# Loading the second chunk of gate's weights one job earlier, in a retention and SwiGLU kernel on one core

## The chip, the cores and the metric

The kernel runs on one core of one Trainium2 chip. The time is device microseconds of one execution; the figure for a kernel is the median of several executions. TensorE is called PE in the profile, its weight loads PEld, VectorE DVE, ScalarE ACT, GpSimd POOL, and the engine that issues most DMAs SP.

## What is computed

The reference is a retention block (8 batches, 8 heads, 576 positions, 64 per head) whose output, laid out as 4608 tokens by 512, goes through an RMS norm and a SwiGLU feed-forward of width 1536.

```python
scores = scale * np.matmul(q, k.transpose(0, 1, 3, 2))
Dmat = np.where(rel >= 0, gamma[:, None, None] ** rel[None, :, :], 0.0)
attn_out = np.matmul(scores * Dmat[None], v)
x = attn_out.transpose(0, 2, 1, 3).reshape(B * S, H * D)
rms = np.sqrt(np.mean(x * x, axis=-1, keepdims=True) + 1e-06)
xn = x / rms * rms_g
g = xn @ w_gate
out = (g * (1 / (1 + np.exp(-g))) * (xn @ w_val)) @ w_out
```

All arithmetic is float32, but the three weight matrices arrive as 64-bit floats. The kernel rounds them to float32 itself.

## The kernel before

**Stages.** The attention is cut into jobs: one pair of heads of one batch, or of a part of one batch. Jobs 0 to 3 cover batch 0, jobs 4 to 7 the first 192 positions of batch 1. `start()` (L977) does these eight jobs, and then the feed-forward of the first two blocks of 384 tokens with plain matmuls (`up_plain`, L640; then `across`). After that, ten further blocks are computed with a seven-product scheme, among which the remaining attention jobs are slipped in. All of the change is in `start()`.

**One job.** In the loop over `j` in `start()`, `slot(j)` issues, in this order: PE's values of job `j-1` (L390), scores and states of job `j` (L307, L329), VectorE's weighting `ret` (L342) and running sums (L364, L366), and then the carried part of job `j-1` on PE (L412) with its result into `x` on VectorE (L435). Then `turn(j+1)` transposes the next job's q and k on PE (L247, L241) and copies them out on ACT (L252); `scale_v` scales v on ACT (L285); `square` (ACT L477) and `gather` (DVE L487) collect the sum of squares of the tokens. Job 5 ends with `norm_1(0)`: matmuls `ms` (PE L499), `r` (DVE L504) and a power on POOL (L505); then `diagonals` (DVE L547). Job 6 ends with `norm_2(0)`: `rb` (PE L562) and four L564 on VectorE, which give block 0's normalised `x`. The order written in the source is the order on every engine. A small memset `tick` on POOL (L401) stands between PE's values and carried parts of each job.

**Loads.** SP issues all loads of jobs 0 to 7 ahead of the job loop, job by job: q (L169), k and v (L177, two DMAs each), and for the first jobs the tails (L210). Eight semaphores are used in turn by SP's DMAs, so each of them is issued only once the eighth before it has landed. `load_chunks(n)` (L857 issues) loads weight chunks up to number `n`, in between.

**Weights.** A chunk is 512 rows by 256 columns of gate's or val's weights, 1 MB of 64-bit words. Chunks 0 and 1 are the two halves of the first third of gate, 2 and 3 those of val, and so on; after twelve of these come six of `w_out`. A chunk is first put in a spare place (in `w_out`, which is not yet in use, or in `w_gate`), and is then rounded on VectorE and ACT: `exponent` (DVE L874), then three passes on ACT (L890), which `act()` issues one at a time; the mantissa in three operations (DVE L901, L906, and L911, which needs the last ACT pass and ends the use of the spare place); and `join` (DVE L919), after which the chunk can be used. `rounding()` is a generator that goes through these operations chunk by chunk, one to a step. `weights(n)` takes `n` steps of it. Its step after L911 of chunk `i` also calls `load_chunks(i + 5)`, for chunk 1 that is chunks 4 and 5. For chunks from the second on, the exponent of the following chunk is taken ahead, before the join or before the mantissa, if its load has been issued.

Before the job loop three steps are taken, for chunk 0. In the loop, the numbers of steps by job are written by hand. Steps 4 and 5 end chunk 0; 6 to 9 are L874, L901, L906 and L911 of chunk 1; 10 is L874 of chunk 2; 11 is L919 of chunk 1.

**First matmuls of the feed-forward.** `up_plain(0, 0, 0)` has four groups of matmuls (L652, 128x384, four matmuls or eight records each). The first two read chunk 0, the last two chunk 1. Behind the first group stand values and carried part of job 7, its square and `gather`, and `weights(2)`; behind the second `norm_1(1)`, behind the third and fourth the rest of block 1's norm.

Of the kernel before, what the change touches and what calls it, by code (L numbers as in the profile page):

```python
# [41 lines left out]
def kernel(  # L42
# [11 lines left out]
    nc = tc.nc  # L54
# [104 lines left out]
    def load_first(j, tails):  # L159

        b, hp, *_ = jobs[j]
        d = st[j]
        tiles = tiles_of(j)[1]
        room = h_of[0].rearrange("p f t -> p (f t)")
        part = room[:, j * 4 * P : j * 4 * P + tiles * P]
        d["q"] = part.rearrange("p (e t d) -> p e t d", e=2, d=D)
        nc.sync.dma_start(  # L169
            out=part.rearrange("p (e t) -> p e t", e=2),  # L170
            in_=q[b, 2 * hp : 2 * hp + 2, : tiles * P].rearrange("e (p t) d -> p e (t d)", p=P),
        )
        for nm, src in (("k", k), ("v", v)):
            t = first_places[nm][j][:, : tiles * P].rearrange("p (c e d) -> p c e d", e=2, d=D)
            d[nm] = t
            for e in range(2):
                nc.sync.dma_start(  # L177
                    out=t[:, :, e],
                    in_=src[b, 2 * hp + e, : tiles * P].rearrange("(c p) d -> p c d", p=P),
                )  # L180
            for n in (0, 1) if nm == "k" else (2,):
                load_tails(b, n, tails)
# [50 lines left out]
    def turn(j):  # L233

        d = st[j]
        n = tiles_of(j)[1]
        for nm in "qk":
            ps = bank(f"turn_{j}_{nm}")
            for c in range(n):
                if nm == "k":  # L240
                    nc.tensor.transpose(  # L241
                        out=ps[:, c * P : c * P + P],
                        in_=d["k"][:, c].rearrange("p e d -> p (e d)"), identity=ident,
                    )
                    continue
                for e in range(2):
                    nc.tensor.matmul(  # L247
                        ps[side(e), c : n * P : n], lhsT=d["q"][:, e, c], rhs=ident,
                        start=True, stop=True,
                    )  # L250
            t = d[nm + "T"] = att.tile([P, S], F32, tag=nm + "T", name=f"{nm}T_{j}")
            nc.scalar.copy(out=t[:, : n * P], in_=ps[:, : n * P])  # L252
        if jobs[j][3] < NC:
            return
        last = bank(f"turn_{j}_t")
        for i, nm in enumerate("qk"):
            o = slice(i * TAIL, i * TAIL + TAIL)
            nc.tensor.transpose(
                out=last[:, o], in_=d[nm + "t"].rearrange("p e d -> p (e d)"),
                identity=ident[:TAIL, :TAIL],  # L260
            )
        for i, nm in enumerate("qk"):
            o = slice(i * TAIL, i * TAIL + TAIL)
            nc.scalar.copy(out=d[nm + "T"][:, NFULL * P :], in_=last[:, o])
# [13 lines left out]
    def scale_v(j):  # L278
        d = st[j]
        hp = jobs[j][1]  # L280
        i0, i1 = tiles_of(j)
        for e in range(2):
            tails = [d["vt"][:, e]] if "vt" in d else []
            for t in [d["v"][:, i0:i1, e]] + tails:
                nc.scalar.activation(  # L285
                    out=t, in_=t, func=AF.Copy, scale=gv[: t.shape[0], hp, e : e + 1]
                )
# [154 lines left out]
    def slot(j, rest=True):  # L442

        if j > len(jobs):
            return
        if rest and j > 0:
            values(j - 1)
        if j < len(jobs):
            scores(j)
            states(j)  # L450
        if j < len(jobs):
            weigh(j)
        if j < 2 * NHP:
            sums(j)
        if rest and j > 0:
            carried(j - 1)
        if 2 * NHP <= j < len(jobs):
            sums(j)
# [16 lines left out]
    def square(u, c):  # L475
        t = temp(f"sq_{u}_{c}")
        nc.scalar.activation(out=t, in_=x_of[u][:, c], func=AF.Square)  # L477
        return t

    def gather(u, c, sq):  # L480

        if c == NHP - 1 and u > 2:
            nc.vector.scalar_tensor_tensor(
                out=t_of[u], in0=t_of[u], scalar=EPS * DM / P, in1=sq, op0=ALU.add, op1=ALU.add
            )
        elif c:
            nc.vector.tensor_tensor(out=t_of[u], in0=t_of[u], in1=sq, op=ALU.add)  # L487
        else:
            t_of[u] = sq
# [5 lines left out]
    def norm_1(u):  # L495

        ms = bank(f"ms_{u}")
        for s in range(NS):
            nc.tensor.matmul(  # L499
                ms[:, s : s + 1], lhsT=t_of[u][:, s * P : s * P + P], rhs=mean_w,  # L500
                start=True, stop=True,
            )
        r = tmp.tile([P, NS], F32, tag="r", name=f"r_{u}", bufs=1)
        nc.vector.tensor_scalar(out=r, in0=ms[:, :NS], scalar1=EPS, scalar2=None, op0=ALU.add)  # L504
        nc.gpsimd.tensor_tensor(out=r, in0=r, in1=mhalf.to_broadcast([P, NS]), op=ALU.pow)  # L505
        t_of[u] = r
# [36 lines left out]
    def diagonals(u):  # L543
        r = t_of[u]
        t_of[u] = temp(f"diag_{u}")
        for s in range(NS):
            nc.vector.tensor_scalar(  # L547
                out=t_of[u][:, s * P : s * P + P], in0=ident, scalar1=r[:, s : s + 1],
                scalar2=None, op0=ALU.mult,
            )  # L550
# [290 lines left out]
    def spare(i):  # L841

        return i % 4 if i < n_up else LATER[i - n_up]

    def load_chunk(i, queue):
        dst, src, rws, cols = chunks[i]
        if src.dtype != F32:
            n = dst.shape[1]
            cols = slice(2 * (cols.start or 0), 2 * cols.stop if cols.stop else None)
            src = src.bitcast(U32)  # L850
            at = spare(i)
            dst = free[:, : 4 * DM] if at == 3 else (
                w_out[:, 4 * at : 4 * at + 4].rearrange("p c f -> p (c f)")
            )
            dst = words_of[i] = dst.bitcast(U32).rearrange("p (c f) -> p c f", c=n)
            waits_at[at] = i
        queue.dma_start(out=dst, in_=src[rws, cols].rearrange("(c p) f -> p c f", p=P))  # L857
        there_at[i] = now + 3 if now else 0

    def load_chunks(n, queue=nc.scalar):  # L860

        nonlocal n_loads
        while n_loads < min(n, len(chunks)) and waits_at.get(spare(n_loads)) is None:
            load_chunk(n_loads, queue)
            n_loads += 1
# [21 lines left out]
    def act(n=0, chunk=-1):  # L887

        while acts and (n > 0 or acts[0][0] <= chunk):
            nc.scalar.activation(func=AF.Relu, **acts.pop(0)[1])  # L890
            n -= 1
# [70 lines left out]
    def weights(n):  # L962

        for _ in range(n):
            next(steps, None)
# [11 lines left out]
    def start():  # L977
# [5 lines left out]
        def table(i, queue):  # L983
            t, values_ = tables[i]
            src = nc.inline_tensor(values_, name=t.tensor.name + "_table")
            queue.dma_start(out=t, in_=src.ap())
# [12 lines left out]
        for j in range(2 * NHP):  # L999
            load_first(j, {0: range(2), 1: range(2, H)}.get(j))  # L1000
            if j == 1:
                table(3, nc.sync)
            load_chunks((1, 1, 1, 1, 2, 2, 2, 3)[j], nc.sync)
        table(4, nc.sync)
        nc.sync.dma_start(out=rms_g, in_=moe_rms_g.rearrange("(c p) -> p c", p=P))
        load_chunks(4, nc.sync)
# [20 lines left out]
        for j in range(2 * NHP):  # L1027
            slot(j)
            if j + 1 < 2 * NHP:
                turn(j + 1)  # L1030
            if squares:
                gather(*squares.pop())
            for i in ((1,), (2,), (3,), (4, 5), (6,), (7,), (), ())[j]:
                scale_v(i)
            if j:
                u, c = divmod(j - 1, NHP)
                squares.append((u, c, square(u, c)))
            act(1)
            if j == 5:
                norm_1(0)  # L1040
            elif j == 6:
                norm_2(0)
            weights((2, 0, 0, 1, 1, 1, 1, 0)[j])
            if j == 4:
                gather(*squares.pop())
            elif j == 5:
                diagonals(0)
            act(1)
# [130 lines left out]
```

## Time and profile before

| | |
|---|---|
| median of 9 executions | 1136.57 us |
| lowest and highest | 1135.36 and 1137.64 us |
| the profiled execution | 1136.57 us, span 1134.8 us |
| granted PE clock, mean over the span | 0.994 |
| PE busy | 1116.2 us, 98% |
| VectorE busy | 732.8 us, 65% |
| ACT busy | 258.7 us, 23% |
| DMA | 126.73 MB, mean 112 GB/s |

Times in the profile count from the start of the span, which is 1.8 us shorter than the execution's time. The page divides the span into 40 slices of 28.4 us; each digit is the busy share in tenths, and PEclk is the clock granted to PE in the same way. The waits view lists who waited, for whom, and the total, the number and the longest of these waits. The chain of waits follows the work that ended last back from its end: start, duration, and what it was. A wait that is called "issue" is one that no semaphore explains.

### The profile page before, as it was taken

What the parts mean: (1) busy time and instruction counts of PE and PEld (TensorE: products, weight loads), DVE (VectorE), ACT (ScalarE), POOL (GpSimd) and SP (SyncE); (2) the same over time, 40 slices, a digit from 0 to 9 for tenths busy, and PEclk for the clock granted to TensorE, in tenths of its full rate; (3) what the DMA queues carried; (4) which work ended last, traced back from release to release, by engine and by line L of the source; (5) the groups of instructions that cost most, each with busy time, mean ns of one, the idle gap of its engine ahead of it and who ended that gap; (6) DMA issues with size and microseconds to landing.
All of it is one profiled execution on the core that took longest, in us unless ns stands there. A gap on an engine that the chain in (4) does not pass through costs nothing.

```text
span 1134.8 us, 24783 instructions
## 1 busy us (share of the span) xinstructions
PE 1116.2 (98%) x10454; PEld 1042.2 (92%) x10454; DVE 732.8 (65%) x1452; ACT 258.7 (23%) x508; POOL 40.5 (4%) x68
## 2 busy tenths in 40 slices
PE   7899999999999999999999999999999999999998
PEld 6655567999999999999999999999999999999998
DVE  5788989655775784485677585465676666446352
ACT  5465551011212211211211121121120210120110
POOL 0000000460000000000000000000000000000000
PEclk8899999999999999999999999999999999999999
DMA  8744568336254374063553555215536503303304
GB/s 201 227 134 145 140 152 243 62 64 157 68 141 109 101 166 136 1 130 80 119 127 49 136 146 102 113 53 101 138 69 136 156 5 99 126 1 101 123 1 112
DMA packets 307040, 126.73 MB, mean 112 GB/s; under 512 B 284528, under 2 KB 289904, under 8 KB 306928
## 3 DMA queue, kind: packets, MB, share of 16 engines
q1 hardware_dynamic: 302640, 123.66, 42.8%
q8 instruction: 82, 1.34, 0.5%
q10 hardware_dynamic: 4288, 1.48, 0.5%
q14 instruction: 30, 0.25, 0.1%
HBM read 110.14 MB, written 14.94 MB: 110 GB/s over the span
## 4 chain that ended last, share of the span: by engine, by line
PE 96%; DVE 1%; DMA 1%; issue 1%; ACT 1%; SPq 0%; POOL 0%; POOLq 0%; ACTq 0%
PE x L595 14%; PE w L595 14%; PE z L595 14%; PE up L652 11%; PE xo L726 8%; PE wo L726 8%; PE zo L726 8%; PE y L595 7%; PE yo L726 4%; PE av L390 2%; PE av L412 2%; PE s L307 2%; PE s L329 1%; PE ms L513 1%; DMA w_val<-in_v_dram 0%
## 5 line engine op out<-in xcount | busy, mean ns | idle before, releaser
L619 ACT COPY m<-x 128x384 f32<-128x384 f32 x60 | 28.7, 479 | 338.4 <-PE x L595 338.4
L726 PE MATMUL xo<-h,w_out 128*128 128x192 f32 x528 | 90.3, 328 | 0.0
L595 PE MATMUL x<-x,w_gate 128*128 128x192 f32 x480 | 88.8, 328 | 0.2 <-issue 0.2
L595 PE MATMUL w<-sums,w_val 128*128 128x192 f32 x480 | 88.6, 328 | 0.3
L595 PE MATMUL x<-x,w_val 128*128 128x192 f32 x480 | 88.7, 328 | 0.0
L595 PE MATMUL w<-sums,w_gate 128*128 128x192 f32 x480 | 87.9, 326 | 0.0
L595 PE MATMUL z<-x,w_gate 128*128 128x192 f32 x480 | 87.8, 326 | 0.0
L595 PE MATMUL z<-x,w_val 128*128 128x192 f32 x480 | 87.8, 326 | 0.0
L726 PEld LDWEIGHTS xo<-h,w_out 128*128 128x128 f32 x528 | 85.9, 190 | 0.6
L726 PE MATMUL wo<-h,w_out 128*128 128x192 f32 x504 | 85.6, 326 | 0.4 <-DVE c_last L774 0.4
L602 DVE TENSOR_TENSOR u<-m,y 128x384 f32<-128x384 f32 x60 | 33.1, 552 | 79.1 <-PE y L595 79.1
L726 PEld LDWEIGHTS wo<-h,w_out 128*128 128x128 f32 x504 | 82.4, 190 | 0.7 <-DVE c_last L774 0.7
L595 PEld LDWEIGHTS w<-sums,w_val 128*128 128x128 f32 x480 | 79.2, 190 | 2.7 <-DVE c L602 2.7
L595 PEld LDWEIGHTS x<-x,w_gate 128*128 128x128 f32 x480 | 79.2, 190 | 1.0 <-issue 0.5
L595 PEld LDWEIGHTS x<-x,w_val 128*128 128x128 f32 x480 | 79.2, 190 | 0.6
L595 PEld LDWEIGHTS z<-x,w_gate 128*128 128x128 f32 x480 | 79.7, 190 | 0.0
L595 PEld LDWEIGHTS z<-x,w_val 128*128 128x128 f32 x480 | 79.6, 190 | 0.0
L595 PEld LDWEIGHTS w<-sums,w_gate 128*128 128x128 f32 x480 | 79.5, 190 | 0.1
L602 DVE TENSOR_TENSOR h<-u,w 128x384 f32<-128x384 f32 x60 | 33.0, 550 | 69.5 <-PE w L595 69.5
L614 ACT ACTIVATE h<-h 128x384 f32<-128x384 f32 x90 | 47.0, 523 | 88.6 <-DVE h L602 88.6
L652 PE MATMUL up<-x,w_gate 128*128 128x384 f32 x192 | 63.8, 489 | 1.7 <-DVE r L504 1.0
L652 PE MATMUL up<-x,w_val 128*128 128x384 f32 x192 | 63.2, 488 | 0.0
(189 smaller groups left out, 1777.2 us busy)
## 6 DMA issues: line engine op xcount, KB each, us to landing
w_out<-w_blocks SPq DMA_DIRECT2D x70, 768.0 KB, 4.8
out_dram<-o SPq DMA_DIRECT2D x364, 24.0 KB, 1.6
qraw<-in_q_dram SPq DMA_DIRECT2D x96, 72.0 KB, 2.6
kraw<-in_k_dram SPq DMA_DIRECT2D x96, 72.0 KB, 2.7
k<-in_k_dram SPq DMA_DIRECT2D x48, 128.0 KB, 2.9
v<-in_v_dram SPq DMA_DIRECT2D x48, 128.0 KB, 3.0
w_out<-in_moe_w_gate_dram SPq DMA_DIRECT2D x5, 1024.0 KB, 5.4
w_out<-in_moe_w_val_dram SPq DMA_DIRECT2D x3, 1024.0 KB, 5.1
```

The lines of the kernel that those rows point to most:

```text
L307: nc.tensor.matmul(s[side(odd), e, i * L : i * L + L], lhsT=d["kT"][side(e), c * L : c * L + L], rhs=d["qT"][side(e), c * L : c * L + L], ...
L329: nc.tensor.matmul(o[side(e)], lhsT=d["k"][side(odd), i, e], rhs=d["v"][side(odd), i, e], start=True, stop=True,)
L390: mm = nc.tensor.matmul(av[odd][column(j, odd, e), i * L : i * L + L], lhsT=d["v"][side(odd), i, e] if c < NC - 1 else d["vt"][:, e], rhs= ...
L412: mm = nc.tensor.matmul(av[odd][column(j, odd, e), i * L : i * L + L], lhsT=d["sum"][c - 1][side(e)], rhs=d["qT"][side(e), c * L : c * L + L],
L513: nc.tensor.matmul(s, lhsT=ones, rhs=y, start=True, stop=True)
L595: nc.tensor.matmul(ps[:, i * HU : i * HU + HU], lhsT=w_up[m][:, 2 * blk + c, cut], rhs=t_of[u][blk][:, c], start=(start and i == c == 0), ...
L602: nc.vector.tensor_tensor(out=o, in0=a, in1=pairs_of(ps), op=ALU.add)
L614: nc.scalar.activation(out=o, in_=c, func=AF.Silu)
L619: nc.scalar.copy(out=s1, in_=pairs_of(x_))
L652: nc.tensor.matmul(ps[:, :U], lhsT=w_up[m][:, 4 * half + c, i * P : i * P + P], rhs=x_of[u][:, c], start=(c == 0), stop=(c == NHP - 1),)
L726: nc.tensor.matmul(ps[:, i * HU : i * HU + HU], lhsT=a[:, c, i * P : i * P + P], rhs=rhs[:, c], start=(start and i == c == 0), stop=False, ...
```

## The change

Two tuples of numbers in `start()` are changed. The first says up to which chunk SP has loaded behind job `j`'s loads: chunk 1 is now issued behind job 3's loads, ahead of job 4's five DMAs, and no longer behind job 4's. The second gives the rounding steps by job:

| job | steps before | steps after |
|---|---|---|
| 0 | 4, 5 | 4, 5 |
| 2 | none | 6 (L874 of chunk 1) |
| 3 | 6 (L874 of chunk 1) | 7, 8 (L901, L906) |
| 4 | 7 (L901) | 9 (L911, and the loads of chunks 4 and 5) |
| 5 | 8 (L906) | 10 (L874 of chunk 2) |
| 6 | 9 (L911, and the loads of chunks 4 and 5) | none |

The steps that are taken behind the first `up` group are then 11 and the following one, where they were 10 and 11.

```diff
@@ -1000,7 +1000,7 @@
             load_first(j, {0: range(2), 1: range(2, H)}.get(j))
             if j == 1:
                 table(3, nc.sync)
-            load_chunks((1, 1, 1, 1, 2, 2, 2, 3)[j], nc.sync)
+            load_chunks((1, 1, 1, 2, 2, 2, 2, 3)[j], nc.sync)
         table(4, nc.sync)
         nc.sync.dma_start(out=rms_g, in_=moe_rms_g.rearrange("(c p) -> p c", p=P))
         load_chunks(4, nc.sync)
@@ -1040,7 +1040,7 @@
                 norm_1(0)
             elif j == 6:
                 norm_2(0)
-            weights((2, 0, 0, 1, 1, 1, 1, 0)[j])
+            weights((2, 0, 1, 2, 1, 1, 0, 0)[j])
             if j == 4:
                 gather(*squares.pop())
             elif j == 5:
```

## The prediction

> **What bounds the kernel now.** I read the page first: its first two sections say that TensorE is the limit nearly everywhere.
>
> ```profile
> PE 1116.2 (98%) x10454; PEld 1042.2 (92%) x10454; DVE 732.8 (65%) x1452; ACT 258.7 (23%) x508; POOL 40.5 (4%) x68
> PE   7899999999999999999999999999999999999998
> PEclk8899999999999999999999999999999999999999
> ```
>
> PE has idle time to give back only in the first two or three slices (28.4 us each), and only there is its clock below full. That is the attention stage of jobs 0 to 7 and the first matmuls of the up projection, where the change acts. From 63.19 us on, the chain of waits shows one unbroken run of `up` matmuls (69.93 us long): whatever starts that run earlier shortens the kernel by the same amount, and nothing else there does. So I read PE's waits from 20 to 64 us, and the chain of waits over the same stretch.
>
> ```profile
> PE turn_k L241 <- issue: 2.2, 1, 2.2
> PE up L652 <- DVE r L504: 1.0, 1, 1.0
> PE up L652 <- DVE x L564: 0.7, 1, 0.7
> ```
>
> ```profile
> 30.93 2.17 issue
> ...
> 49.30 1.13 DVE w_gate L911
> ...
> 55.16 0.35 DVE w_gate L919
> 55.51 0.70 issue
> ```
>
> The chain names L911 and L919: the third mantissa step and the joining of gate's second chunk (chunk 1). L911 stands at 49.3 us, between block 0's normalisation and job 7's `ret`; L919 runs 55.07 to 56.29, and the third group of `up` matmuls, the first to read that chunk, starts at 56.44. The wait is booked on L504, a tiny operation that is queued behind L919 on VectorE. The 2.17 us of "issue" at 30.93 is a wait of PE that no semaphore explains. The DMA view has the stretches around it: from 27.7 to 30.5 us the engines move 369 GB/s, which is chunk 1 (issued 25.15), and no packet of the instruction queue q8 starts; in 30.5 to 31.7 the same view has
>
> ```profile
> q8 instruction: 1, 0.02, 5.6%
> ```
>
> The page has 82 packets on q8 for 20,908 PE and PEld records, 255 for each, so q8 looks like PE's own code, and I read the stall as code waiting behind chunk 1. The windows show what it cost besides:
>
> ```profile
> 25.83:29.25 3.42, 3.02 (x126) 2.61 (x126) 2.12 (x10) 3.08 (x9) 0.09 (x1) 1.00 0.89 261
> 29.25:32.66 3.41, 1.68 (x39) 1.25 (x33) 3.09 (x11) 0.37 (x1) 0.00 (x0) 1.00 1.03 256
> 32.66:36.07 3.41, 2.87 (x71) 2.46 (x72) 1.78 (x6) 2.41 (x7) 0.09 (x1) 0.50 0.54 125
> 36.07:39.49 3.42, 3.42 (x46) 2.64 (x46) 2.84 (x11) 0.97 (x2) 0.00 (x0) 0.50 0.54 123
> ```
>
> Columns: window, PE, PEld, DVE, ACT, POOL, clock, DMA share, GB/s. After a stretch in which PE was busy 1.68 of 3.41 us, the clock is 0.50 for 6.83 us.
>
> **The change part by part.** VectorE's rounding steps, with durations from the timeline: L874 0.69 us, L901 0.68, L906 1.21, L911 1.22, L919 1.22. No arithmetic is added or removed; the steps move.
> Before: job 3 L874, job 4 L901, job 5 L906, job 6 L911, first `up` group L874 of chunk 2, then L919.
> After: job 2 L874, job 3 L901 and L906, job 4 L911, job 5 L874 of chunk 2, job 6 none, first `up` group L919, then L874 of chunk 3.
>
> *Job 2.* L874 (0.69) goes into an idle gap of VectorE, 28.12 to 29.20 (1.08 us, waiting for PE L329). It now waits for chunk 1: issued at 21.50 in the place of job 4's q, landing 5.6 us later as before, at 27.1. VectorE is free for it at 28.12 and would end at 28.81, 0.4 us before PE has job 3's states ready; a landing up to 28.5 costs nothing. If it is later, job 3's `ret` is queued behind it, one for one.
>
> *Job 3.* 1.89 us replaces 0.69. VectorE is busy until 33.84, then L874, then idle 1.68 until job 4's `ret` at 36.12. The two steps end at about 35.7, so they just fit, but they also cap the gain: however early PE comes, job 4's `ret` starts no sooner than 35.7.
>
> *Job 4.* L911 for L901, after 39.2, in the gap where VectorE waits 1.10 us for ACT's square until 40.95. L911 needs the third L890 pass of ACT (1.15 us each); the three now stand behind jobs 2 and 3's squares and end by 37.8. Ends at 40.4: hidden.
>
> *Job 5.* L874 of chunk 2 (0.69) for L906 (1.21), between `r` at 42.92 and `diag` at 44.96, which waits for POOL's power anyway. It now needs chunk 2, issued 36.83 plus 5.6, or 42.4. Covered; `diag` is queued behind it if it lands late.
>
> *Job 6.* L911 is gone from the chain: -1.13 us at job 7's `ret`. But PE is then in the first `up` group until 50.96 and started job 7's values at 50.89, so PE gains at most the 0.28 us wait on the tick. What remains is that VectorE comes 1.1 us earlier to the last square and to L919.
>
> *Joining.* L919 then runs about 53.6 to 54.8 instead of 55.07 to 56.29, and the third `up` group follows the `ms` matmuls at 55.44 rather than 56.44: -1.0 us. Next late is `rb`, which stands on PE behind that group and the fourth (16 records, 5.40 us together), while its input `diag` ends at 58.45, some 2.4 us before: hidden. The 0.7 us after `rb` stays.
>
> *SP's queue.* Chunk 1's issue (0.47 us) passes five DMAs of job 4 (q, two k, two v). They leave 0.5 us later and behind 1 MB: chunk 1's own time at 369 GB/s is 2.8 us. What stood behind chunk 1 before (job 5) landed 5.5 us after issue, so q of job 4 at 21.97 lands by about 27.5, k by 28.5, v by 29.5. PE needs q at 30.02 and k at 30.60: about 2 us of slack. One later DMA waits for chunk 1's landing either way (SP's wait of 1.1 us at L177). Step 9 also issues chunks 4 and 5, now in job 4: chunk 5 leaves once L911 is done, at about 40.4 instead of 50.46. Behind it on SP are job 8's q and k, first used at 115 us. Nothing on POOL is passed.
>
> *The code stall.* Chunk 1's burst, 27.3 to 30.2, moves to about 23.6 to 26.5, and the fetch after 27.7 meets job 4's and 5's small loads instead. From its packet (after 30.5) to PE's restart at 33.10 were about 2.5 us; PE ran from 27.7 to 30.93 on what it had. So a fetch that starts at once leaves no stall, one that starts 1 to 2 us late leaves 0.3 to 1.6. Bounds: 0 to 2.2 us saved; I take half, 1.1, because the engines stay busy. If the clock also stays full, PE is ready before VectorE's cap and job 4 gains 0.4. The following chain then holds no half clock: gather, L911 (39.6) and job 5's `ret` at 40.15 instead of 41.42, -1.27. If the clock still halves, PE's `carried` and `turn` set the order and it is -0.7. Between the two, -0.95, which then carries through `r`, POOL, `diag` and L564 to the first `up` group.
>
> Two rules of the Trainium skill bear on this. In "DMA: Bandwidth & Descriptors", section "Queues, rings and completion order", an engine is said to alternate between queues packet by packet; then the code was not held up by chunk 1 as a whole, moving it would save nothing at 30.93, and the sum would be 1135.6 instead of 1134.6. In "TensorE: Matmul & The Clock Gate", section "HAM oscillation", only PE gaps over about 3.4 us are said to throttle; by that the clock would not have halved here, while the rows above show it did after a gap of 2.17.
>
> **Sum.** The profiled execution took 1136.57 us (span 1134.8), which is also the median of the nine runs. 1136.57 - 1.0 (joining) - 0.95 (job stage) = 1134.6.
>
> **Rivals.** *Only the joining is gained.* The code stall stays or moves by as much, VectorE's chain from 39 us is unchanged: 1136.57 - 1.0 = 1135.6. For it: the fetch falls in busy DMA stretches in both orders. *The change does nothing that counts.* Chunk 1 lands after 28.5, or chunk 2 after 43.7, and VectorE waits in order with `ret` or `diag` behind it; at 1 us late the joining's gain is used up: 1136.6, and at 2 us 1137.5. For it: one chunk in this trace took 11.0 us to land; against: that one stood behind two others. *Slower.* The code packet that started at about 23.6 now falls into chunk 1's burst. PE passed 27.7 with the code that came with it; with 2.5 us from packet to use, it decides from a start after 25.2. A hold-up like the present one (2.9 us after 23.6) starts it at 26.5: a stall of 1.3 in the dense stretch of jobs 2 and 3, the clock halved one window earlier (half of 3.41, 1.7 more) and, with the present stall kept, 1.3 + 1.7 + 0.5 for k arriving behind = 3.5, less the joining: 1139.1. Against: chunk 1's first packets came 1.1 us after issue and its bulk only after 2.2, at about 23.6, when the code packet is already starting.
>
> **How the numbers follow.** Forecast (1134.0 to 1135.2, or with no stall at all and the tick and power waits shortened too, 1133.4) 0.58; only the joining 0.20; nothing 0.10; slower 0.12. A measurement of this kernel tells 0.2%, 2.27 us, from no change: the border lies at 1134.3. Some 0.27 of the forecast's chance is beyond it, since its full sum without any stall is 1.27 + 1.0 = 2.27; the rest, the joining and the nothing case make 0.62; slower, from the last rival, 0.11. The range runs from 1133.4 to 1137.5, leaving out the slower rival and little more.
>
> **What would show it.** Right: L919 of chunk 1 ends before the `ms` matmuls do, and no wait of PE before the third `up` group; PE's "issue" wait near 31 us is shorter than 2.17; the unbroken `up` run starts near 61.2 instead of 63.19; L874 of chunk 1 at about 28.1 with no wait. Wrong: an "issue" wait of PE at 27 to 29 us with a clock of 0.50 after 29.25, or VectorE waiting for w_out's DMA in job 2 or 5 with `ret` or `diag` late; a time above 1137.5 or below 1133.4.

## The result, and the profile after

The changed kernel takes 1141.09 us (median of 9 executions, 1138.66 to 1142.78) against 1136.63 us of the kernel before (29 executions, 1134.61 to 1138.05): a ratio of 1.0038, 95% interval 1.0029 to 1.0046. It is slower by about 4.5 us, above the predicted range of 1133.4 to 1137.5. The profiled execution took 1138.88 us (span 1137.1), so it lies at the lower end of this kernel's times, and 2.3 us above the profiled one of before.

The page after, the same lines that were shown of before. They hardly tell where 2.3 us went:

```profile
PE 1116.4 (98%) x10454; PEld 1042.1 (92%) x10454; DVE 732.1 (64%) x1452; ACT 258.9 (23%) x508; POOL 39.4 (3%) x68
PE   7899998999999999999999999999999999999998
PEclk8899999999999999999999999999999999999999
```

One digit differs in PE's row: an 8 in the seventh slice, 171 to 199 us. First the early part, where the change acts. PE's waits of the changed kernel from 20 to 64 us, as far as they answer to those of before:

```profile
PE av L390 <- issue: 1.0, 1, 1.0
...
PE up L652 <- DVE x L564: 0.7, 1, 0.7
...
PE turn_k L241 <- issue: 0.4, 1, 0.4
```

The wait of 1.0 us before the third `up` group is gone, as forecast. The wait of 2.17 us at 30.93 is gone too, but two others called "issue" have come, 0.99 us at 27.88 and 0.4 us at 32.14. The chain of waits shows what is left of it at the start of the unbroken `up` run, which was at 63.19 before:

```profile
27.88 0.99 issue
...
46.35 1.28 PE rb L562 x2
...
56.41 5.27 PE up L652 x16
61.68 0.66 PE rb L562 x2
62.36 0.62 DVE x L564
63.03 12.20 PE up L652 x37
```

Only 0.16 us was gained. The clock tells the rest. Windows of the changed kernel (columns as in the prediction); it is 1.00 in the windows from 28.15 to 41.82 us, where before it was 0.50 from 32.66 to 39.49:

```profile
41.82:45.24 3.42, 2.80 (x55) 2.49 (x56) 2.59 (x13) 1.67 (x2) 1.28 (x2) 0.50 1.00 367
45.24:48.66 3.42, 3.42 (x46) 2.01 (x44) 1.81 (x6) 2.56 (x5) 0.09 (x1) 0.50 1.05 392
```

The half clock of 6.83 us has not gone but moved, to where `rb` for block 0 runs. `diag` started 1.04 us sooner (43.92 against 44.96), but `rb` took 1.28 us and L564 waited 1.58 us for it, because PE's transposes ahead of it and `rb` itself ran at half the clock (`rb` 1.49 us in PE's timeline for 0.81 before), and the first `up` group started 1.0 us later than before (49.12 against 48.11 in PE's timeline).

The loss lies 110 us further on, where the diff changes nothing. `h` (L658) is there VectorE's product of gate's part with the result of an `up` group for val; PE waits for it before a later group. PE's waits from 130 to 192 us: before has only the second of these lines.

```profile
PE up L652 <- DVE h L658: 2.9, 1, 2.9
PE av L412 <- POOL tick L401: 0.3, 1, 0.3
```

The chain of waits of the changed kernel through the same stretch, read downwards, says why `h` was late:

```profile
156.03 1.24 DVE w_gate L911
157.29 0.38 SPq L857
157.66 0.04 issue
157.71 6.32 DMA qraw<-in_q_dram
...
166.13 2.30 DMA vt<-in_v_dram
168.46 0.35 ACT vt L285
...
170.46 1.16 ACT w_gate L890
171.64 1.23 DVE w_gate L911
172.86 0.47 DVE h L658
173.34 0.04 issue
173.38 10.59 PE up L652 x32
```

SP stood still until 157.29 because its next instruction was the load of the last chunk (chunk 17, the sixth of `w_out`), whose spare place L911 of chunk 16 frees at 157.27. All loads of job 11 (qraw, kraw, k, v, vt) stood behind it. ACT then waited for v and vt, with the L890 passes of chunk 17 behind those in its order; L911 of chunk 17 waited for these passes (VectorE stood idle for 4.29 us), and `h`, which PE needs, stood behind L911 on VectorE. In SP's timeline of before, job 11 went first and the same chunk last:

```profile
153.78 1.97 SPq L156 DMA_DIRECT2D qraw<-in_q_dram  x4
...
160.01 1.12 SPq L229 DMA_DIRECT2D vt<-in_v_dram  x1
161.23 0.54 SPq L857 DMA_DIRECT2D w_gate<-in_moe_w_out_dram  x1
```

There, too, an L911 that waited for ACT stood in front of an `h`, but one `up` group later in the order, and PE did not wait for it. VectorE's timeline of before:

```profile
170.52 1.22 DVE L911 SCALAR_TENSOR_TENSOR w_gate<-w_gate 128x1024 uint32<-128x1024 uint32 x1 [1.38 <-ACT w_gate L890]
171.66 0.54 DVE L658 TENSOR_TENSOR h<-h,up 128x384 f32<-128x384 f32 x1
```

The first `xo` matmul (L726, a product with `w_out`), the end of this stage, came at 185.70 before and at 188.18 after: 2.48 us, the whole difference of the two spans and a little more.

The reason is in the sum of the second tuple. Jobs 0 to 7 took 6 steps of the rounding before and take 7 now. Behind every `up` group `weights(2)` goes on from there, so from the first group on the whole rounding runs one step ahead. A load of a chunk is issued in the step of an L911, behind it, and so the order of SP's queue changes. Compared over the whole kernel it differs in two places: at chunk 1, which the diff names, and at chunk 17, which changed places with job 11. That is the theory (**step lead**); the rivals in the experiments were that the loss comes from the early part (a code wait, the half clock), and that the order on SP alone makes it.

### The profile page after: what moved, and what is told of

Its sections match the earlier page's. It is cut to its first block, busy times and chain, and to the rows that moved or that the text cites. A ratio compares the mean times of both kernels' runs of the same rounds, so it can differ in the third digit from the quotient of the medians.

```text
span 1137.1 us, 24781 instructions
## 1 busy us (share of the span) xinstructions
PE 1116.4 (98%) x10454; PEld 1042.1 (92%) x10454; DVE 732.1 (64%) x1452; ACT 258.9 (23%) x508; POOL 39.4 (3%) x68
## 4 chain that ended last, share of the span: by engine, by line
PE 94%; DMA 2%; DVE 1%; ACT 1%; issue 1%; SPq 1%; POOL 0%; POOLq 0%; DVEq 0%; ACTq 0%
PE x L595 14%; PE w L595 14%; PE z L595 14%; PE up L652 9%; PE xo L726 8%; PE wo L726 8%; PE zo L726 8%; PE y L595 7%; PE yo L726 4%; PE av L390 2%; PE s L307 1%; PE av L412 1%; PE s L329 1%; DMA qraw<-in_q_dram 1%; PE ms L513 1%
## 5 line engine op out<-in xcount | busy, mean ns | idle before, releaser
L619 ACT COPY m<-x 128x384 f32<-128x384 f32 x60 | 28.7, 479 | 338.3 <-PE x L595 338.3
L726 PE MATMUL xo<-h,w_out 128*128 128x192 f32 x528 | 90.3, 328 | 0.0
L726 PEld LDWEIGHTS xo<-h,w_out 128*128 128x128 f32 x528 | 85.9, 190 | 0.6
L726 PE MATMUL wo<-h,w_out 128*128 128x192 f32 x504 | 85.6, 326 | 0.4 <-DVE c_last L774 0.4
L726 PEld LDWEIGHTS wo<-h,w_out 128*128 128x128 f32 x504 | 82.5, 190 | 0.7 <-DVE c_last L774 0.7
```

Source lines behind the costliest of these rows:

```text
L619: nc.scalar.copy(out=s1, in_=pairs_of(x_))
L726: nc.tensor.matmul(ps[:, i * HU : i * HU + HU], lhsT=a[:, c, i * P : i * P + P], rhs=rhs[:, c], start=(start and i == c == 0), stop=False, ...
```

## The experiments

Every ratio is to runs of the kernel before on the same chip, taken together with the run. "Run starts" is the start of the unbroken `up` run in the profiled execution (63.19 before, 63.03 after).

| run | median us (n) | before | ratio, 95% interval | run starts | late wait of PE for `h` |
|---|---|---|---|---|---|
| e1_after_job11_first | 1138.59 (12) | 1136.99 | 1.0017, 1.0008 to 1.0027 | 62.27 | 1.8 |
| e2_before_job11_last | 1139.80 (11) | 1136.99 | 1.0024, 1.0015 to 1.0033 | 63.35 | 1.7 |
| e3_after_step_back | 1137.44 (11) | 1136.99 | 1.0003, 0.9993 to 1.0012 | 63.33 | none |
| e4_load_only | 1136.38 (11) | 1136.99 | 0.9995, 0.9987 to 1.0004 | 63.50 | none |
| e5_before_step_ahead | 1142.24 (6) | 1136.85 | 1.0042, 1.0027 to 1.0058 | 65.55 | 3.1 |
| e6_steps_no_load | 1136.60 (12) | 1136.85 | 1.0000, 0.9990 to 1.0009 | 63.67 | none |
| e7_load_one_step_each | 1136.92 (12) | 1136.85 | 1.0000, 0.9991 to 1.0008 | 63.04 | none |
| e8_change_again | 1140.06 (6) | 1136.85 | 1.0032, 1.0019 to 1.0044 | 63.05 | 3.0 |
| e9_load_later | 1134.59 (11) | 1137.42 | 0.9978, 0.9969 to 0.9986 | 61.19 | none |
| e10_steps_hold | 1136.11 (11) | 1137.42 | 0.9996, 0.9987 to 1.0004 | 61.35 | none |
| e11_before_hold | 1137.76 (12) | 1137.42 | 1.0009, 0.9998 to 1.0020 | 62.24 | none |
| e12_later_and_steps | 1136.89 (12) | 1136.84 | 1.0006, 0.9997 to 1.0015 | 65.53 | none |
| e13_load_later_again | 1135.16 (11) | 1136.95 | 0.9986, 0.9977 to 0.9995 | 61.36 | none |
| e14_load_two_later | 1136.81 (11) | 1136.95 | 1.0002, 0.9993 to 1.0011 | 63.08 | none |

### Is it the step lead? Two ways to take it out

**The changed kernel with the lead taken back** behind the first `up` group, so that everything later is as before and the early part as changed:

```diff
-                    weights(2)
+                    weights(2 if now > 1 else 1)
```

> The changed kernel, but one rounding step fewer behind the first up group (1 in place of 2), so that from there on the rounding steps stand at the same places as in the kernel before, and chunk 17's load is again behind job 11's loads. Late-queue theory: 1135.5 to 1137, as in the run with job 11's loads moved. Job-stage theory: 1140 to 1142.

The late wait is gone and so is the loss: 1.0003, no difference. SP's order from the first `up` group on is that of before. This is also the worth of the early part by itself: nothing that can be measured, with the "issue" waits at 1.58 us (28.22) and 0.65 us (33.08) and the run of `up` starting at 63.33.

**The changed kernel with job 11's loads ahead of chunk 17 again**, the lead kept:

```diff
-                elif step == at + 3:
+                if step == at + (2 if i == 2 else 3):
```

> The changed kernel, but job 11's loads are issued one group earlier, so that on SP's queue they stand ahead of chunk 17's load again, as before the change; everything else, the first 60 us included, is the changed kernel's. Late-queue theory (the loss is that chunk 17's load, which waits for L911 of chunk 16, went ahead of job 11's loads and made PE wait 2.9 us at 170.5): PE's wait there is gone and the time falls from 1141.1 to 1135.5 to 1137, since the joining's gain of 1 us is still there. Job-stage theory (the loss is in the first 60 us, from chunk 1's load in the way of PE's code and the half clock): stays at 1140 to 1142.

About half comes back (1.0038 to 1.0017); the time stays above the 1135.5 to 1137 that was expected. The order on SP is therefore not all of it. VectorE's timeline shows the other half, columns start, duration, operation, and the idle time before it with what ended it:

```profile
164.49 0.69 DVE L874 TENSOR_SCALAR w_gate<-w_gate 128x1024 uint32<-128x1024 uint32 x1 [3.49 <-DMA w_gate<-in_moe_w_out_dram]
...
169.79 1.23 DVE L911 SCALAR_TENSOR_TENSOR w_gate<-w_gate 128x1024 uint32<-128x1024 uint32 x1 [1.47 <-ACT w_gate L890]
170.94 0.55 DVE L658 TENSOR_TENSOR h<-h,up 128x384 f32<-128x384 f32 x1
```

Now the chunk itself is late (issued 159.16 instead of 157.29), and L874 of chunk 17, one step ahead, asks for it at 161.0. L911 is again in front of an `h` that PE needs, and PE waits 1.8 us.

### Does the lead make the kernel before slow?

**The kernel before with chunk 17 ahead of job 11** on SP, no lead:

```diff
-                elif step == at + 3:
+                elif step == at + (4 if i == 2 else 3):
```

> The kernel before, with one thing changed: job 11's loads are issued one group later, so that chunk 17's load goes ahead of them on SP's queue, as in the changed kernel. The first 60 us are untouched. Late-queue theory: 1139 to 1141.5, with the wait of PE before a group of up matmuls near 171 us. Job-stage theory: 1136.6, as before.

Slower by 0.24%, with a late wait of 1.7 us and the first `xo` 2.6 us later: the order alone costs something. With the 0.17% of e1, where the lead is there without the order, that makes about the whole 0.38%; as chunk 17 itself comes later in e1, this split is an estimate.

**The kernel before with one step more** behind the first `up` group:

```diff
-                    weights(2)
+                    weights(2 if now > 1 else 3)
```

> The kernel before, with one rounding step more behind the first up group (3 in place of 2). Jobs 0 to 7 are untouched; from the first up group on, the rounding runs one step ahead, as in the changed kernel, and chunk 17's load goes ahead of job 11's loads. Late theory (the loss comes from this lead of one step alone, through SP's queue and through L911 of chunk 17, which then waits for ACT in front of an earlier group's h): the whole late loss, PE waiting 2.5 to 3 us near 171 us, 1139.5 to 1141. Queue-only theory: 1139 to 1140, the same as with job 11's loads put behind chunk 17. Job-stage theory: 1137.

Slower by 0.42%, 1.2 us above the expected range, with this wait of PE after 130 us:

```profile
PE up L652 <- DVE h L658: 3.1, 1, 3.1
```

This number is not the lead's alone: in its profile the run of `up` also starts 2.4 us late (65.55). Of that 1.5 us were there before the extra step, at block 0's L564 (48.64 against 47.12, behind a code wait of 2.8 us), where the two kernels have the same order; the rest came in the groups after it. The late wait, though, is that of the changed kernel, without any of its tuples.

**The changed kernel once more**, for its spread:

> The changed kernel once more, for a second profile: the profiled execution was among the shortest of its kernel (1138.9 beside a median of 1141.1). If the rest of the loss is the clock that halves after PE's wait near 171 us in a part of the executions, a profile near the median shows a clock of 0.50 for some us after that wait, or one more such stretch before 63 us; the times by granted clock fall into two groups.

1140.06, 1.0032. Its profiled execution took 1140.89 us, 2.0 longer than the first one, with the same late wait (3.0 against 2.9). The windows tell the two apart, this run's first and the earlier profile's below:

```profile
174.90:178.40 3.50, 3.50 (x7) 1.93 (x6) 3.30 (x12) 1.50 (x4) 0.00 (x0) 0.51 0.89 279
```

```profile
174.90:178.40 3.50, 3.50 (x13) 2.04 (x12) 3.30 (x12) 1.50 (x4) 0.00 (x0) 1.00 0.94 305
```

After the same wait the clock was halved for one window in one execution and not in the other, and 7 `up` records ran in it instead of 13. Half of 3.5 us is 1.75, about the difference. The nine timed executions fit this: those with a mean granted clock of 0.994 to 0.996 took 1138.66 to 1139.98, those with 0.990 to 0.993 took 1141.09 to 1142.78. So the first `xo` comes 2.5 us late in the first profile and 4.4 in the second (190.05 against 185.70 before). That the halving is what parts the times was seen in these two profiles only, and the six executions of this run (1137.92 to 1142.38) part less clearly.

### Where did the forecast's two gains go?

**The load alone**: the kernel before with the changed first tuple. The stall of code was to shrink, the joining to stay as it was.

> Half of the change: chunk 1 is loaded behind job 3's loads, the rounding steps by job are those of the kernel before. The late queue is as before. Late-queue theory: 1136 to 1137.5, the load's move is nearly free. Job-stage theory: at least half of the loss, 1138.5 to 1141, with PE's issue wait near 27.7 us and a clock of 0.50 behind it.

No difference (0.9995). The code wait is 1.52 us at 27.95 instead of 2.17 at 30.93, and the half clock lies in two single windows, 30.3 to 33.7 and 43.9 to 47.4.

**The steps alone**, in as many steps as before, so that there is no lead:

```diff
-            weights((2, 0, 0, 1, 1, 1, 1, 0)[j])
+            weights((2, 0, 0, 2, 1, 1, 0, 0)[j])
```

> The kernel before with its loads untouched and six rounding steps in jobs 0 to 7 as before, but placed 2, 1, 1 in jobs 3, 4, 5 (L874 and L901; L906; L911) in place of 1, 1, 1, 1 in jobs 3 to 6. So L911 leaves job 6, and nothing moves from the first up group on. If the joining's gain is real: L919 ends before the ms matmuls, PE's wait before the third up group falls from 1.0 us to nearly nothing, 1135.6 to 1136.3. If it is eaten in the job stage by the way steps stand there: 1137 or more.

The wait before the third `up` group is down to 0.2 us, and the time is the same: 1.0000. In its profile the clock is half from 32.8 to 36.2 and from 43.0 to 49.9, 3.4 us more of it than before, and the run starts at 63.67. Its executions lie in two groups, 1134.7 to 1136.1 and 1137.1 to 1138.6.

**Load and steps**, again 6 steps: first tuple as changed, second `(2, 0, 1, 1, 1, 1, 0, 0)`.

> Chunk 1 loaded behind job 3's loads as in the change; the same six steps as before, one each in jobs 2, 3, 4 and 5 (L874, L901, L906, L911). Nothing moves from the first up group on; job 3 holds one step, not two. If the chunk's packets in front of PE's code are what ate the early gain: 1136.5 to 1138, PE idle near 27.9 or 31 us, as in the changed kernel with the step back. If it was the two steps in job 3 in front of job 4's ret: 1135.0 to 1136.0.

The wait before the third group is down to 0.2 us, the code wait is 1.19 us (28.23), the clock is half from 30.4 to 33.8 and from 44.0 to 47.4: 1.0000 once more. Three kernels with the join's wait gone or nearly so and no lead (e3, e6, e7) are all at no difference.

**With the clock held.** To see the joining without the moving clock, two small matmuls are added on PE behind `turn(j + 1)` of jobs 3 to 6. They write to a bank of their own and nothing reads it. First the kernel before with them, as a control, then the one with the moved steps (e6):

```diff
+            if 3 <= j < 7:
+                hold = bank(f"hold_{j}")
+                for _ in range(2):
+                    nc.tensor.matmul(hold[:, :P], lhsT=ones, rhs=ones, start=True, stop=True)
```

> The kernel before with the same unused matmuls of ones in jobs 3 to 6: the control. Clock theory: 1136.0 to 1136.8, a little under before, and 0.5 to 1 us over the kernel with the steps moved. Otherwise: 1136.9 to 1137.4.

> The kernel with steps 2, 1, 1 in jobs 3, 4, 5 and untouched loads, plus two matmuls of ones (128x128 by 128, result unused) on PE behind the transposes in jobs 3 to 6, where PE waits for ACT's copies. Clock theory (the joining's 1 us is taken back in the executions in which PE's clock halves again between 42 and 50 us): the clock stays full there in all or most executions, and the time is 1135.0 to 1135.8. If the clock is not what takes it back: 1136.6 to 1137.2, the two matmuls costing up to 0.5.

In both the clock is full in all windows from 15.6 to 49.7 us. A code wait of 2.3 us remains in the control, and the clock stays full in spite of it. The starts of the run of `up` in the two chains, the control's and then the moved steps':

```profile
62.24 12.85 PE up L652 x39
```

```profile
61.35 13.81 PE up L652 x42
```

They are 0.89 us apart. The code wait is 0.5 us shorter in the second (1.8 for 2.3), but that is not where it comes from: the first `up` group starts at 47.15 in both, and the third at 55.49 and 54.60, with a wait of 1.00 us before it in the control and of 0.16 in the other. In these two profiles the joining is thus worth nearly the 1.0 us of the forecast. The medians are 1.65 us apart, but the intervals overlap, against the kernel before neither differs, and the control came out above what was expected of it either way. As a gain of the kernel's time it is likely, not settled.

### The load the other way

If a code packet is held up by a chunk's burst, then a chunk that is issued later should let it through. **One job later**, with chunk 1's first two steps both in job 4:

```diff
-            load_chunks((1, 1, 1, 1, 2, 2, 2, 3)[j], nc.sync)
+            load_chunks((1, 1, 1, 1, 1, 2, 2, 3)[j], nc.sync)
-            weights((2, 0, 0, 1, 1, 1, 1, 0)[j])
+            weights((2, 0, 0, 0, 2, 1, 1, 0)[j])
```

> The opposite of the change: chunk 1 is loaded one job later than before (behind job 5's loads), and its first step, L874, is taken in job 4 together with L901 (steps 2, 1, 1 in jobs 4, 5, 6); nothing moves from the first up group on. Code theory (PE's fetch of its own code stands behind a chunk's packets): the fetch that PE needs at 30.9 us now comes before the chunk's burst, and the issue wait there falls from about 2.2 to 2.7 us to under 1; if nothing else takes its place, 1135.3 to 1136.2. If the wait is not the chunk's doing: still 2 us or more, and 1136.9.

> The kernel with chunk 1 loaded one job later than before (L874 and L901 in job 4), once more. If its gain belongs to the load's place: again 1133.8 to 1135.3, faster than before by 0.1 to 0.3%, and PE's issue wait at 31 us under 1.5. If it was luck of that run: 1136 to 1137, and a wait near 2.

1134.59 (0.9978) and, run again, 1135.16 (0.9986): both intervals lie below 1, so this version beats both kernels. Chunk 1 is issued at 27.85, and the code packet that began at 30.57 before now begins at 28.45, ahead of the burst. PE's chain at the place of the old stall:

```profile
30.99 0.91 issue
...
61.19 14.13 PE up L652 x43
```

0.91 us for 2.17, the clock half for one window (42.2 to 45.6) instead of two, and the run 2.0 us sooner, though L911 is still in job 6 and the wait before the third group still there (0.8). L874 was moved along with the load, and no run moves it alone, so that the gain is the load's is argued from the shorter code wait and not shown by itself.

**Two jobs later**, first tuple `(1, 1, 1, 1, 1, 1, 2, 3)`, the same steps:

> Chunk 1 loaded behind job 6's loads, two jobs later than before and three later than in the change, with L874 and L901 in job 4 as in the run above. Code theory: the fetch asked for near 27.7 us meets only small packets, it starts before 29.5 and PE's issue wait at 31 us is 0.3 to 1.2; the fetch after 33 us may be held instead, but PE needs that one later. Time 1134 to 1135.5. If the wait does not follow the load: still near 2 us, and 1136 to 1137.

The code wait shrinks further, to 0.36 us at 31.20. But the time is that of before (1.0002), not the 1134 to 1135.5 expected with so short a wait. VectorE now waits for the chunk in job 4, and the clock is half for two windows again (40.6 to 47.5); which of the two takes the gain back is not shown:

```profile
DVE w_gate L874 <- DMA w_out<-in_moe_w_gate_dram: 1.5, 1, 1.5
```

**One job later with the join freed too**, steps `(2, 0, 0, 0, 2, 2, 0, 0)`:

> Chunk 1 loaded one job later than before, as in the run with the late load, and L911 taken in job 5 behind L906 (steps 2, 2 in jobs 4, 5), so that it leaves job 6; nothing moves from the first up group on. If the joining's wait (0.8 us in that run) is still to be had: PE's wait before the third up group is gone, the unbroken run of up matmuls starts near 60.4 us and the time is 1133.4 to 1134.4. If L911 in front of diag costs what it saves, or the clock takes it back: 1134.4 to 1135.4.

A miss: 1.0006. L911, now in job 5, waits for ACT's third pass, in front of `diag`, which the norm of block 0 needs:

```profile
45.38 1.23 DVE L911 SCALAR_TENSOR_TENSOR w_gate<-w_out,w_gate 128x1024 uint32<-128x1024 uint32 x1 [1.61 <-ACT w_gate L890]
46.52 0.67 DVE L547 TENSOR_SCALAR diag<-ident,r 128x128 f32<-128x128 f32 x3
```

In its profile the code packet began only at 31.30, inside the burst, though the load stands where it stood in e9. Whether that belongs to this kernel or to that execution stays open.

## Why the prediction was wrong

**The step that failed** is the first one: "whatever starts that run earlier shortens the kernel by the same amount, and nothing else there does". It took the stage behind the first `up` group for unchanged, and followed step 9's chunks 4 and 5 and job 8's q and k, but no further. The step table had 7 steps where there had been 6, so each later step stands one place earlier in VectorE's, ACT's and SP's order. At chunk 17 this puts a load that waits for a place in front of loads that need not wait, and an L911 in front of an earlier `h`; PE then waited 2.9 us at 170.5. Two runs with the early load and without the lead (e3, e7) are at no difference, and the two that put one or both of these into the kernel before (e2, e5) are slower by 0.24 and 0.42%. No rival had this mechanism; that the slower one's 1139.1 lies near the profiled 1138.88 is chance, since its 3.5 us were to be lost before 63 us, where 0.16 were gained.

The miss is 6.5 us (1141.09 against 1134.6). About 4 of them are the lead (1.0038 with it, 1.0003 without). The rest is the forecast's two gains in the early part, 1.95 us together, of which e3 shows nothing in the time.

**Joining, -1.0.** Right as a mechanism: the third group follows the `ms` matmuls with no wait. L919 ended at 55.82 instead of 56.29, not 54.8. In the changed kernel's profile it gave 0.03 us (the third group at 56.41 instead of 56.44), since the first group started 1.0 us later; with the clock held, 0.89 us (e10 and e11).

**The job stage, -0.95.** As far as `diag` the size came out: it started 1.04 us sooner. But that is luck in part. Half of it was there at `r` (42.42 instead of 42.92); the other half came in POOL's power, 1.24 us instead of 1.77, for which the sum had no term. PE's two "issue" waits together are 0.8 us shorter than the one of before (0.99 and 0.38 for 2.17; the prediction took 1.1), but they do not lie where the forecast put them: the slower rival's mechanism came true in this profile. The packet that began at 23.64 began at 26.27 (the rival: 26.5). In the stretch from 22.5 to 26.2 us the DMA view of the changed kernel shows the engines at 318 GB/s and no packet of q8; in 26.2 to 27.2 it has

```profile
q8 instruction: 1, 0.02, 6.7%
```

PE then waited at 27.88, 0.99 us for the predicted 1.3. "Against" that rival the prediction put that chunk 1's bulk would come only at about 23.6, "when the code packet is already starting". The times of the burst were right: the DMA engines rise to over 370 GB/s at about 23.6, and the chunk lands at 26.95 (forecast 27.1). What failed is the race that was called from a difference of nothing: the packet, due at 23.64, began when the chunk was nearly in. It does not always come out so. In e1, which is the changed kernel up to its late loads, a q8 packet began at 24.75, in the middle of chunk 1's burst, there was no wait near 28 us, and PE waited 1.3 us further on, ahead of 31.66. The DMA view of e1 from 24.5 to 25.5 us:

```profile
DMA packets 189, 0.40 MB, mean 401 GB/s; under 512 B 0, under 2 KB 0, under 8 KB 188
q8 instruction: 1, 0.02, 5.7%
```

The rival was wrong in keeping the stall at 30.93 as well (0.4 us of it was left, at 32.14), and so in its price. The prediction's bounds for a late fetch hold a slip: with 2.5 us from packet to use, a fetch 2 us late leaves 27.7 + 2 + 2.5 - 30.93 = 1.3 us and not 1.6.

**The clock.** The prediction let the half clock go or shrink with the stall. In the changed kernel's profile it lay at the norm of block 0 (41.8 to 48.7), where the sum had no term for it, and cost there what the chain up to `diag`, 1.04 us ahead, had won. That the change put it there is not shown: in e2 and e5, which are the kernel before up to the first `up` group, it lies at 35.0 to 38.4 and 45.2 to 48.6, and at 34.8 to 38.2 and 45.0 to 48.4, where the profile of before has it once, from 32.7 to 39.5. Its place also changes from one execution to the next.

**The steps moved.** Job 2's L874 ran at 27.95 with no wait; job 4's L911 ended at 40.54 (forecast 40.4); job 5's L874 cost nothing, as said. Job 3's two steps ended at 36.92, not 35.7, because `ret` of job 3 was at 30.42 instead of 29.20, and job 4's `ret` stood directly behind them.

**The two rules weighed.** In the Trainium skill, "DMA: Bandwidth & Descriptors", section "Queues, rings and completion order", a DMA engine is said to take turns between queues packet by packet, by which the chunk would not hold the code up as a whole. Here a q8 packet began 2.6 us later when the chunk's burst was moved in front of it, and 2.1 us earlier when the burst was moved behind it (e9), which is more than the rule leads one to expect. But in e1 and e12 a packet began while the burst ran, at 401 and 389 GB/s in the microsecond around it, which agrees with the rule; what parts the two cases no run shows. In "TensorE: Matmul & The Clock Gate", section "HAM oscillation", the rule is put as no PE-idle gaps over about 3.4 us. Here the clock was half for a window after a wait of 3.0 us (e8), and with waits of at most 1.0 us from 20 to 48 us in the changed kernel; in the kernel before it was half from 32.66 on, 1.7 us into the wait of 2.17 and not after it. So by these profiles shorter gaps go with a halved clock too.

## What to carry to other kernels

When a step of work whose order is written by hand is moved, compare the order on every engine from there to the end of the kernel, the DMA issuer's first: a generator that is one step ahead stays ahead, and here its cost came 110 us after the edit. A load that must wait for a buffer belongs behind the loads that need not wait, and work that only has to be done some time belongs behind what the limiting engine waits for. A bulk load can have a neighbour that no semaphore shows, the code of a busy engine: look at the instruction queue's packets before and after such a move, in more than one execution. Expect a gain of 1 us in a stage of light PE load to be overrun by where the half clock falls, which one profile of each kernel does not settle.

## What the runs showed of the hardware

- A 16 KB packet of the instruction queue met chunk 1's burst in thirteen of the sixteen profiles. In eleven of them it began within a microsecond of the end of the burst (26.27 in the changed kernel, 30.57 before); in e1 (24.75) and e12 (31.30) it began in the middle of it. In the three in which the burst came behind (e9, e13, e14), it began at 28.4 to 28.7. PE restarted 2.3 to 3.5 us after the packet in all of them (30.57 to 33.10 before, 26.27 to 28.87 after, 28.45 to 31.90 in e9). That these packets are PE's code is worked out from their number and from these waits.
- The clock was halved in stretches of 3.4 or 6.8 us, whose place changed between 30 and 52 us from profile to profile, also where the early part was the same (32.7 to 39.5 before, 34.8 to 38.2 and 45.0 to 48.4 in e5). With two unused 128x128 matmuls per job it was 1.00 from 15.6 to 49.7 us in the two profiled executions, even with a code wait of 2.3 us left in.
- The same wait of 3 us at 170.5 was followed by a half clock in one execution and by a full one in another.
